# A second expert unit taken straight from SBUF: direct products, outer x sums first, operand streams fetched ahead (fp32 attention, then four experts)

## The chip, the cores and the metric

One core of a Trainium2 chip. The metric is the device time of one execution in microseconds (us); most executions of a kernel agree within 0.3%. A ratio is the mean time of one kernel's fast runs over that of the other's of the same rounds, so it isn't quite the ratio of the medians quoted beside it.

## The reference, cut to what matters

```python
# lightning attention in blocks of 64, with a running state per head
out = intra + inter            # q, k, v: (4, 8, 768, 64) fp32
x = attn_out.transpose(0, 2, 1, 3).reshape(3072, 512)

p = domain_probs / (domain_probs.sum(-1, keepdims=True) + 1e-09)
for e in range(4):             # four experts, all of them on all tokens
    h = np.maximum(x @ w1[e], 0.0)          # 3072x512 @ 512x1024
    out += p[:, e:e + 1] * (h @ w2[e])      # 3072x1024 @ 1024x512
```

## The kernel before

The tokens are taken in three groups g of 1024, and a *unit* (g, e) is one group through one expert. Unit by unit, the second product of one unit (h @ w2) is interleaved on TensorE with the first product (x @ w1) of the next, and with the attention of the next group. Below, "unit 0", "unit 1" and so on without a pair of numbers are the steps of this main loop: unit 0 does the second product of (0,0) and the first of (0,1).

Every product is a Strassen product in Winograd's form: seven products M1 to M7 for eight. The left operands are A11, A12, A22 and the sums S1 to S4 of w1, the right ones B11, B21, B22 and the sums T1 to T4 of x. For the first product this is done twice, an outer level and an inner one. The inner sums are made by GpSimd (w1) and VectorE or GpSimd (x), stored to HBM, and read back as streams:

```python
    def inner(eng, what, to, blk, ops, at):        # four inner sums of one block, then stores
        s = stage.tile([P, 4, 256], FP32, name="ops", tag="st")
        for i, (name, x, y, op) in enumerate(ops):
            b[name] = s[:, SLOT[name]]
            tt(eng, b[name], b[x], b[y], op)
        stores.append(lambda: (
            nc.scalar.dma_start(out=to[:, 0], in_=blk[:, 0, 0:256]),
            nc.scalar.dma_start(out=to[:, 1:5], in_=s[:]),
            nc.scalar.dma_start(out=to[:, 5:7], in_=...), made.add(what)))
    # `stage` has 7 buffers of 4 KB per partition: raw w1 and w2, their sums, x sums, inner sums.

    def feed(g, e, m):                             # both streams of one outer product
        xs = stream.tile([P, 7, 256], FP32, name="xs_in", tag="x")
        nc.sync.dma_start(out=xs[:], in_=x_ops[g, MS.index(m)])
        ws = stream.tile([P, 7, 256], FP32, name="ws_in", tag="w")
        nc.sync.dma_start(out=ws[:], in_=w1_ops[e, MS.index(m)])

    def first_product(...):                        # 7 inner products x 2 matmuls = 14 per outer product
        ...
                nc.tensor.matmul(out=p[...], lhsT=ws[:, W1_AT[i], ...], rhs=xs[:, X_AT[i]], ...)
            # each inner product is taken out of PSUM on its own: 7 evictions of 128x512
```

The very first unit, (0,0), can't wait for such streams. Its products are *direct*: no inner level, operands as they lie in SBUF.

```python
    def direct_product(m, tags):                   # 4 quarters x 4 matmuls = 16 per outer product
        a, b = w1_now[A_OF[m]], x_now[B_OF[m]]
        ...
        def quarter(at):
            for s in range(2):
                for c in range(2):
                    nc.tensor.matmul(out=p[...], lhsT=a[c][:, f:f + P], rhs=b[:, c, ...], ...)
            # 4 evictions of 128x512

    first, own = prepare_w1(1), [lambda x=x: inner_x(nc.vector, 0, x, x_now[B_OF[x]]) for x in SEQ]
    chores.append(first.pop(0))
    for many in zip(own, first):                   # inner sums of x and of w1 of expert 1
        chores.extend(many)
    sum_x("T1", "B12", "B11")
    for m in SEQ0[2:]:                             # M5, M6, M7, M3, M4 of unit (0,0)
        for x, f in enumerate(direct_product(m, (...))):
            f(); rest()
            if x != 2:
                pump()                             # last chore's stores, then the next chore
        if m == "M5":
            sum_x("T2", "B22", "T1")
        if m == "M6":
            sum_x("T3", "B22", "B12")
            sum_x("T4", "B21", "T2")
```

In the traces of this kernel instructions keep their program order on each engine and each queue (in the prediction, one sum on VectorE has its inputs at 71 us and runs at 96.47, behind others); across engines only data and buffers hold them. A buffer goes to the next tile once the last reader of the old one is done (a sum of the changed kernel stood 8.21 us for that).

## Time and profile before

| | before |
|---|---|
| median of 3 runs | 1282.16 us |
| profiled span | 1281.2 us |
| TensorE weight loads busy | 83% |
| VectorE, GpSimd, ScalarE busy | 62%, 23%, 17% |
| TensorE idle from 70 to 145 us | 35.3 us in three waits |
| TensorE idle after 145 us | 4.0 us in seven waits |

A fp32 matmul of 128x128 by 128x256 stands in the trace as two records 0.216 us apart (eight records in 1.73 us), so one matmul is 0.43 us, and "x32" is 16 matmuls. Idle time before a row stands in brackets at its end, with what ended it. In the rows of 40 slices each digit is a share in tenths: of busy time (PE, TensorE) or of the full clock that TensorE was granted (PEclk). PEld are weight loads, DVE is VectorE, ACT ScalarE, POOL GpSimd, and SPq and ACTq are the transfers issued from the sync and the scalar engine. The lines that carry the argument are in the prediction.

### The profile page before, as it was taken

What the parts mean: (1) busy time and instruction counts of PE and PEld (TensorE: products, weight loads), DVE (VectorE), ACT (ScalarE), POOL (GpSimd) and SP (SyncE); (2) the same over time, 40 slices, a digit from 0 to 9 for tenths busy, and PEclk for the clock granted to TensorE, in tenths of its full rate; (3) what the DMA queues carried; (4) which work ended last, traced back from release to release, by engine and by line L of the source; (5) the groups of instructions that cost most, each with busy time, mean ns of one, the idle gap of its engine ahead of it and who ended that gap; (6) DMA issues with size and microseconds to landing.
All of it is one profiled execution on the core that took longest, in us unless ns stands there. A gap on an engine that the chain in (4) does not pass through costs nothing.

```text
span 1281.2 us, 16185 instructions
## 1 busy us (share of the span) xinstructions
PE 1225.6 (96%) x6348; PEld 1069.5 (83%) x6348; DVE 791.5 (62%) x1288; ACT 216.7 (17%) x361; POOL 295.8 (23%) x286
## 2 busy tenths in 40 slices
PE   6967599999999999999999999999999999999998
PEld 5856488888888888888888888888888888888887
DVE  5669357747746855664674684674674764755742
ACT  2211111211221120221121112021020120220200
POOL 3646156057336840011100062000010000000001
PEclk9998699999999999999999999999999999999999
DMA  9747999599979985665754466545374545454412
GB/s 192 215 188 261 291 334 353 191 353 328 334 286 314 325 299 186 195 235 173 230 172 182 163 226 243 217 151 217 150 257 179 204 166 195 174 186 184 164 53 97
DMA packets 173916, 283.85 MB, mean 222 GB/s; under 512 B 87696, under 2 KB 120592, under 8 KB 173840
## 3 DMA queue, kind: packets, MB, share of 16 engines
q1 hardware_dynamic: 144672, 223.11, 51.7%
q10 hardware_dynamic: 27248, 53.41, 11.3%
q0 software_dynamic: 1920, 6.29, 1.3%
q8 instruction: 50, 0.82, 0.3%
q14 instruction: 26, 0.21, 0.0%
HBM read 223.14 MB, written 59.64 MB: 221 GB/s over the span
## 4 chain that ended last, share of the span: by engine, by line
PE 47%; issue 39%; DVE 4%; DMA 4%; POOL 4%; SPq 1%; ACTq 0%; ACT 0%; POOLq 0%; DVEq 0%
PE q L584 19%; PE pg L532 18%; DVE m L93 2%; PE op L384 2%; PE sp L360 2%; PE pM L633 2%; POOL ops L93 2%; PE kvp L393 2%; PE op L378 1%; DMA w_ops<-w1b 1%; PE kp L337 1%; POOL xo L93 1%; DVE ops L93 1%; PE qp L337 1%; DMA ws_in<-w_ops 1%
## 5 line engine op out<-in xcount | busy, mean ns | idle before, releaser
L532 PE MATMUL pg<-xs_in,ws_in 128*128 128x256 f32 x2156 | 520.4, 381 | 25.1 <-DMA ws_in<-w_ops 21.1
L532 PEld LDWEIGHTS pg<-xs_in,ws_in 128*128 128x128 f32 x2156 | 406.7, 190 | 85.0 <-issue 21.8
L93 DVE TENSOR_TENSOR m<-pg,m 128x512 f32<-128x512 f32 x451 | 307.3, 687 | 90.0 <-PE pg L532 82.8
L584 PE MATMUL q<-w2t,hS 128*128 128x256 f32 x1536 | 360.7, 379 | 0.0
L584 PEld LDWEIGHTS q<-w2t,hS 128*128 128x128 f32 x1536 | 291.1, 190 | 39.3 <-issue 0.2
L600 DVE SCALAR_TENSOR_TENSOR acc<-q,gate,acc 128x256 f32<-128x256 f32 x288 | 138.8, 482 | 238.4 <-PE q L584 238.0
L584 PE MATMUL q<-w2t,m 128*128 128x256 f32 x1152 | 270.9, 379 | 0.0
L584 PEld LDWEIGHTS q<-w2t,m 128*128 128x128 f32 x1152 | 219.3, 190 | 29.9
L544 ACT ACTIVATE m<-m 128x512 f32<-128x512 f32 x132 | 82.7, 630 | 381.1 <-DVE m L93 368.8
L602 POOL DMA_DIRECT2D out_dram<-acc x24 | 13.2, 550 | 579.3 <-DVE acc L600 579.3
L93 DVE TENSOR_TENSOR hS<-m,m 128x512 f32<-128x512 f32 x96 | 73.6, 768 | 26.2 <-ACT m L544 26.2
L540 ACT COPY m<-pg 128x512 f32<-128x512 f32 x88 | 51.4, 585 | 208.8 <-PE pg L532 201.1
L93 DVE TENSOR_TENSOR m<-m,m 128x512 f32<-128x512 f32 x96 | 81.1, 846 | 0.0
L93 POOL TENSOR_TENSOR kn<-kn,s_decay 128x256 f32<-128x256 f32 x40 | 29.7, 763 | 158.3 <-PE kp L337 157.1
L597 DVE TENSOR_SCALAR acc<-q,gate 128x256 f32<-128x256 f32 x48 | 23.1, 482 | 51.6 <-PE q L584 51.6
L486 ACT ACTIVATE m<-m 128x512 f32<-128x512 f32 x48 | 30.1, 630 | 144.8 <-DVE m L93 142.8
L93 POOL TENSOR_TENSOR w2o<-w2b 128x1024 f32<-128x1024 f32 x8 | 19.2, 2408 | 104.4 <-DMA w2b<-in_moe_w_dram 104.4
L633 PE MATMUL pM<-xt,w1o 128*128 128x256 f32 x96 | 24.8, 425 | 14.2 <-DVE xt L93 14.2
L388 ACT COPY xT<-op 128x512 f32<-128x512 f32 x24 | 14.0, 584 | 143.6 <-PE op L384 130.2
L93 DVE TENSOR_TENSOR st<-sp,s_decay 128x512 f32<-128x512 f32 x48 | 30.9, 684 | 10.8 <-PE sp L360 10.7
L633 PEld LDWEIGHTS pM<-xt,w1o 128*128 128x128 f32 x96 | 20.6, 217 | 18.2 <-issue 11.9
L93 DVE TENSOR_TENSOR hS<-hS,m 128x512 f32<-128x512 f32 x48 | 35.0, 730 | 0.4
(65 smaller groups left out, 711.6 us busy)
## 6 DMA issues: line engine op xcount, KB each, us to landing
xs_in<-x_ops SPq DMA_DIRECT2D x77, 896.0 KB, 4.7
ws_in<-w_ops SPq DMA_DIRECT2D x77, 896.0 KB, 7.0
w2t<-w_sums SPq DMA_DIRECT2D x96, 256.0 KB, 6.5
w2t<-in_moe_w_dram SPq DMA_DIRECT2D x72, 256.0 KB, 4.9
w_ops<-ops ACTq DMA_DIRECT2D x28, 512.0 KB, 4.6
x_ops<-ops ACTq DMA_DIRECT2D x21, 512.0 KB, 3.7
w2b<-in_moe_w_dram SPq DMA_DIRECT2D x32, 256.0 KB, 7.5
w_sums<-w2o ACTq DMA_DIRECT2D x16, 512.0 KB, 7.1
```

Of the source, the lines that this page charges most:

```text
L93: eng.tensor_tensor(out=o, in0=a, in1=b, op=op)
L337: nc.tensor.transpose(out=x[:, hp * C:(hp + 1) * C], in_=y[:, 2 * hp:2 * hp + 2].rearrange("p h d -> p (h d)"), identity=ident[:],)
L360: nc.tensor.matmul(out=sp[hd][:, hp * C:(hp + 1) * C], lhsT=hc(kT)[half[hd], hp], rhs=hc(qT)[half[hd], hp], start=True, stop=True,)
L384: nc.tensor.matmul(out=op[half[hd], hp * C:(hp + 1) * C], lhsT=vn[:, 2 * hp + hd], rhs=hc(st[hd])[:, hp], start=(first and hp == 0), stop= ...
L393: nc.tensor.matmul(out=kpv[:, hp], lhsT=kn[:, 2 * hp:2 * hp + 2].rearrange("p h d -> p (h d)"), rhs=vn[:, 2 * hp:2 * hp + 2].rearrange("p ...
L486: nc.scalar.activation(out=o[:], in_=o[:], func=AF.Relu)
L532: nc.tensor.matmul(out=p[:, j * 256:(j + 1) * 256], lhsT=ws[:, W1_AT[i], j * P:(j + 1) * P], rhs=xs[:, X_AT[i]], start=(fresh and j == 0), ...
L540: nc.scalar.copy(out=new[at][:], in_=p[:])
L544: nc.scalar.activation(out=new[at][:], in_=new[at][:], func=AF.Relu)
L584: nc.tensor.matmul(out=p[:, s * DH:(s + 1) * DH], lhsT=h[A_OF[m]][:, c * 256 + s * P:c * 256 + (s + 1) * P], rhs=fed2[g, e, m][uu][:, c], ...
L600: nc.vector.scalar_tensor_tensor(out=o, in0=x, scalar=w, in1=o, op0=ALU.mult, op1=ALU.add)
L633: nc.tensor.matmul(out=p[:, s * 256:(s + 1) * 256], lhsT=a[c][:, f:f + P], rhs=b[:, c, j * 256:(j + 1) * 256], start=(s == 0 and c == 0), ...
```

## The change

The intent: unit (0,1) is made direct as well, so that nothing has to come through HBM before unit (0,2); its raw w1 is loaded and the sums of it are begun during unit (0,0), the inner x blocks are made during unit 0's second product, and all four T sums are made before anything else on VectorE. The streams are asked for one product ahead across the border of two units.

```diff
     sum_x("T1", "B12", "B11")
+    sum_x("T2", "B22", "T1")
+    sum_x("T3", "B22", "B12")
+    sum_x("T4", "B21", "T2")
     for f in between:
         f()
+    chores.extend(lambda n=n: raw_w1(1, n) for n in ("A11", "A12", "A21", "A22"))
+    chores.append(lambda: sum_w1(1, "S1", "A21", "A22", ALU.add))
     for m in SEQ0[2:]:
-        for x, f in enumerate(direct_product(m, (...))):
+        for x, f in enumerate(direct_product(0, m, blocks, (...))):
             f(); rest()
-            if x != 2:
+            if x == 1:
                 pump()
-        if m == "M5": ...                          # T2 here, T3 and T4 after M6
+    own = [lambda m=m: inner_x(nc.vector, 0, m, x_now[B_OF[m]]) for m in SEQ0]
+    w2_steps, w1_steps = prepare_w2(1), prepare_w1(2)
+    chores.extend((                                # done during unit 0
+        lambda: sum_w1(1, "S2", ...), own[0], lambda: sum_w1(1, "S3", ...), own[1], w2_steps[0],
+        lambda: sum_w1(1, "S4", ...), own[2], w2_steps[1],
+        own[3], w2_steps[2], w2_steps[3], own[4], w2_steps[4], w1_steps[0], own[5], *w1_steps[1:3], own[6], *w1_steps[3:],
+    ))
...
+    fill = [(*u, m) for u in units[2:] for m in SEQ]
+    fill2 = [(*u, m) for u in units for m in SEQ2]
     for at, (g, e) in enumerate(units):
-        feed2(g, e, SEQ2[0])
         for i in range(7):
-            if i + 1 < 7:
-                feed2(g, e, SEQ2[i + 1])
+            for _ in range(2 if at + i == 0 else 1):
+                if fill2:
+                    feed2(*fill2.pop(0))
             b = second_product(g, e, SEQ2[i], banks)
-            if ahead:
-                feed(*ahead, SEQ[i])
+            if at == 0:
+                a = direct_product(1, SEQ0[i], blocks, ("g1", "g3"))
+            elif ahead:
                 a = first_product(*ahead, SEQ[i], blocks, ("g1", "g3"))
...
-                if ahead and x == 0 and i + 1 < 7:
-                    feed(*ahead, SEQ[i + 1])
+                if x == 0 and at * 7 + i >= 6 and fill:
+                    feed(*fill.pop(0))
```

Cut: w1 of expert 1 for the later groups is prepared in unit 3, four attention steps go from unit 0 to units 1 and 2, and the loads of two attention chunks go into unit 0.

More of the change, by code (lines that the diff above doesn't have):

```diff
@@ L258, with raw_w1, sum_w1 @@
     make_identity(nc, ident[:])
-    w1_now = {}
-    def raw_w1(name):
+    w1_now = {0: {}, 1: {}}
+    def raw_w1(e, name):
         i, j = int(name[1]) - 1, int(name[2]) - 1
         if name == "A22":
-            w1_now[name] = tuple(small("w1b")[:] for _ in range(2))
+            to = tuple(small("w1b")[:] for _ in range(2))
         else:
             t = stage.tile([P, 2, W], FP32, name="w1b", tag="st")
-            w1_now[name] = t[:, 0], t[:, 1]
+            to = t[:, 0], t[:, 1]
         for c in range(2):
             r = j * 256 + c * P
-            nc.sync.dma_start(out=w1_now[name][c], in_=moe_w1[0, r:r + P, i * W:(i + 1) * W])
-    def sum_w1(name, a, b, op):
-        w1_now[name] = tuple(small("w1o")[:] for _ in range(2))
+            nc.sync.dma_start(out=to[c], in_=moe_w1[e, r:r + P, i * W:(i + 1) * W])
+        w1_now[e][name] = to
+    def sum_w1(e, name, a, b, op):
+        if e == 0:
+            to = tuple(small("w1o")[:] for _ in range(2))
+        else:
+            t = stage.tile([P, 2, W], FP32, name="w1o", tag="st")
+            to = t[:, 0], t[:, 1]
         for c in range(2):
-            tt(nc.gpsimd, w1_now[name][c], w1_now[a][c], w1_now[b][c], op)
+            tt(nc.gpsimd, to[c], w1_now[e][a][c], w1_now[e][b][c], op)
+        w1_now[e][name] = to
     for n in range(4):
         load(n)
-    raw_w1("A21")
-    raw_w1("A22")
-    raw_w1("A11")
+    for name in ("A21", "A22", "A11"):
+        raw_w1(0, name)
     probs = consts.tile([P, NTOK // P, E], FP32, name="probs")
@@ L615, with direct_product @@
     SEQ0 = ("M1", "M2", "M5", "M6", "M7", "M3", "M4")
-    blocks = {}
     x_now = {"B11": b11, "B21": b21, "B12": b12, "B22": b22}
     turns = itertools.count()
-    def direct_product(m, tags):
-        a, b = w1_now[A_OF[m]], x_now[B_OF[m]]
+    def direct_product(e, m, blocks, tags):
+        a, b = w1_now[e][A_OF[m]], x_now[B_OF[m]]
         settle(m, blocks)
@@ L643, in quarter @@
                 nc.scalar.activation(out=new[at][:], in_=new[at][:], func=AF.Relu)
-        return [lambda at=at: quarter(at) for at in ("11", "12", "21", "22")] + [lambda: finished(0, 0, m, blocks, new)]
+        return [lambda at=at: quarter(at) for at in ("11", "12", "21", "22")] + [lambda: finished(0, e, m, blocks, new)]
     pairs = (("s0", "s1"), ("q01", "q02"), ("q11", "q12"))
-    between = []
+    between, blocks = [], {}
     for i in range(CPG + 2):
         if i == 3:
-            sum_w1("S1", "A21", "A22", ALU.add)
-            sum_w1("S3", "A11", "A21", ALU.subtract)
+            sum_w1(0, "S1", "A21", "A22", ALU.add)
+            sum_w1(0, "S3", "A11", "A21", ALU.subtract)
         if i == 4:
-            sum_w1("S2", "S1", "A11", ALU.subtract)
-            sum_w1("S4", "A12", "S2", ALU.subtract)
+            sum_w1(0, "S2", "S1", "A11", ALU.subtract)
+            sum_w1(0, "S4", "A12", "S2", ALU.subtract)
             chores.extend(prepare_w2(0))
@@ L660 @@
         if i == 6:
-            between = direct_product("M1", ("g1", "g3"))
+            between = direct_product(0, "M1", blocks, ("g1", "g3"))
         for f, lag in ((scores, 1), (turn, 0), (values, 2)):
@@ L666 @@
             if i == 7 and lag == 0:
-                between += direct_product("M2", ("g1", "g3"))
+                between += direct_product(0, "M2", blocks, ("g1", "g3"))
             if between:
@@ L672 @@
         if i == 0:
-            raw_w1("A12")
+            raw_w1(0, "A12")
         if i == 6:
@@ L680, in sum_x @@
         tt(nc.vector, x_now[name], x_now[a], x_now[b], ALU.subtract)
-    first, own = prepare_w1(1), [lambda x=x: inner_x(nc.vector, 0, x, x_now[B_OF[x]]) for x in SEQ]
-    chores.append(first.pop(0))
-    for many in zip(own, first):
-        chores.extend(many)
     sum_x("T1", "B12", "B11")
+    sum_x("T2", "B22", "T1")
+    sum_x("T3", "B22", "B12")
+    sum_x("T4", "B21", "T2")
     for f in between:
         f()
+    chores.extend(lambda n=n: raw_w1(1, n) for n in ("A11", "A12", "A21", "A22"))
+    chores.append(lambda: sum_w1(1, "S1", "A21", "A22", ALU.add))
     for m in SEQ0[2:]:
-        for x, f in enumerate(direct_product(m, ("g1", "g3", "q01", "q02", "q11", "q12"))):
+        for x, f in enumerate(direct_product(0, m, blocks, ("g1", "g3", "q01", "q02", "q11", "q12"))):
             f()
             rest()
-            if x != 2:
+            if x == 1:
                 pump()
-        if m == "M5":
-            sum_x("T2", "B22", "T1")
-        if m == "M6":
-            sum_x("T3", "B22", "B12")
-            sum_x("T4", "B21", "T2")
-    for n in range(CPG, CPG + AHEAD):
-        load(n)
+    own = [lambda m=m: inner_x(nc.vector, 0, m, x_now[B_OF[m]]) for m in SEQ0]
+    w2_steps, w1_steps = prepare_w2(1), prepare_w1(2)
+    chores.extend((
+        lambda: sum_w1(1, "S2", "S1", "A11", ALU.subtract), own[0],
+        lambda: sum_w1(1, "S3", "A11", "A21", ALU.subtract), own[1], w2_steps[0],
+        lambda: sum_w1(1, "S4", "A12", "S2", ALU.subtract), own[2], w2_steps[1],
+        own[3], w2_steps[2], w2_steps[3], own[4], w2_steps[4], w1_steps[0], own[5], *w1_steps[1:3], own[6], *w1_steps[3:],
+    ))
     units = [(g, e) for g in range(NG) for e in range(E)]
+    fill = [(*u, m) for u in units[2:] for m in SEQ]
+    fill2 = [(*u, m) for u in units for m in SEQ2]
     steps = attention(1)
     for at, (g, e) in enumerate(units):
-        if g == 0 and e < E - 1:
+        if (g, e) == (0, 1) or (g, e) == (0, 2):
             chores.extend(prepare_w2(e + 1) + prepare_w1((e + 2) % E))
+        if (g, e) == (0, 3):
+            chores.extend(prepare_w1(1))
         ahead = units[at + 1] if at + 1 < len(units) else None
@@ L712 @@
         blocks, banks = {}, {}
-        feed2(g, e, SEQ2[0])
         for i in range(7):
-            if i + 1 < 7:
-                feed2(g, e, SEQ2[i + 1])
+            for _ in range(2 if at + i == 0 else 1):
+                if fill2:
+                    feed2(*fill2.pop(0))
             b = second_product(g, e, SEQ2[i], banks)
             a = []
-            if ahead:
-                feed(*ahead, SEQ[i])
+            if at == 0:
+                a = direct_product(1, SEQ0[i], blocks, ("g1", "g3"))
+                a = a[0:1] + [None] + a[1:2] + [None] + a[2:3] + [None] + a[3:]
+            elif ahead:
                 a = first_product(*ahead, SEQ[i], blocks, ("g1", "g3"))
@@ L724 @@
                 for f in part:
-                    f()
+                    if f:
+                        f()
                 rest()
-                if ahead and x == 0 and i + 1 < 7:
-                    feed(*ahead, SEQ[i + 1])
-                if steps and (x == 5 or (x == 2 and i in (2, 5))):
+                if x == 0 and at * 7 + i >= 6 and fill:
+                    feed(*fill.pop(0))
+                if at == 0 and x == 0 and i < AHEAD:
+                    load(CPG + i)
+                if steps and (at > 0 or i > 1) and (x == 5 or (x == 2 and i in (1, 3, 5) and at > 0)):
                     steps.pop(0)()
```

## The prediction

> **What bounds the kernel now.** I read the page's rows of 40 slices first, then who TensorE waited for, then the stretch with the waits in order of time, then the queue that feeds it.
>
> ```profile
> PE   6967599999999999999999999999999999999998
> PEclk9998699999999999999999999999999999999999
> ```
>
> One slice is 32 us. TensorE is full from the sixth slice on; what can be won without removing matmuls lies in the first five, about 160 us.
>
> ```profile
> PE pg L532 <- DMA ws_in<-w_ops: 21.1, 1, 21.1
> PE pM L633 <- DVE xt L93: 14.2, 2, 11.5
> PE qp L337 <- DMA qn<-in_q_dram: 7.1, 2, 4.7
> PE pg L532 <- DVE m L93: 4.0, 7, 0.9
> ```
>
> These are TensorE's waits over the whole span: total, times, longest. The loads at the start (7.1) are not touched by the change. One wait of 21.1 us for a transfer and two for the outer x sums (11.5 and 2.7) make 35.3 us. The timeline places them:
>
> ```profile
> 72.67 15.77 PE L633 MATMUL pM<-xt,w1o 128*128 128x256 f32 x64 [2.66 <-DVE xt L93]
> 99.98 9.06 PE L633 MATMUL pM<-xt,w1o 128*128 128x256 f32 x32 [11.54 <-DVE xt L93]
> 108.87 7.07 PE L633 MATMUL pM<-xT,w1o 128*128 128x256 f32 x32
> 115.78 7.07 PE L633 MATMUL pM<-xt,w1b 128*128 128x256 f32 x32
> 143.97 3.75 PE L532 MATMUL pg<-xs_in,ws_in 128*128 128x256 f32 x8 [21.12 <-DMA ws_in<-w_ops]
> ```
>
> Columns: start, length, operation and count, and in brackets the idle time before it and who ended it. L633 is the direct product of unit (0,0): M5 and M6 in the first row, then M7, M3, M4. L532 is the first product of unit (0,1) from operands that went through HBM. From 72.67 to 143.97, 71.3 us, TensorE does only five direct products.
>
> The sync queue's view of the same stretch says why the transfer is late:
>
> ```profile
> 98.77 0.37 SPq L176 DMA_DIRECT2D w1b<-in_moe_w_dram  x1
> 122.22 0.37 SPq L103 DMA_DIRECT2D qn<-in_q_dram  x1
> 134.96 0.36 SPq L467 DMA_DIRECT2D ws_in<-w_ops  x1
> ```
>
> The queue issues nothing between 99.1 and 122.2, then the attention loads and the w2 blocks, and only at 134.96 the operands that TensorE needs. Ahead of that, GpSimd and VectorE must make inner operand blocks of w1 and x, and the scalar queue must store them. VectorE's own lines show that the 11.5 us are no dependency but a place in a queue:
>
> ```profile
> 71.38 1.23 DVE L93 TENSOR_TENSOR xt<-xT 128x1024 f32<-128x1024 f32 x1
> 93.02 1.80 DVE L93 TENSOR_TENSOR ops<-xT 128x256 f32<-128x256 f32 x2
> 94.86 1.69 DVE L93 TENSOR_TENSOR ops<-xT,ops 128x256 f32<-128x256 f32 x2
> 96.47 3.35 DVE L93 TENSOR_TENSOR xt<-xT 128x1024 f32<-128x1024 f32 x1
> ```
>
> The T3 sum at 96.47 has had its inputs (xT) since 71, but stands behind `ops` work in VectorE's order.
>
> **What the Trainium skill says.** "Perfetto Trace Analysis", section Identifying the Most-Contended Engine: matmul busy time is a poor measure of headroom; weight-load busy time is a better one. The trace agrees and gives the scale:
>
> ```profile
> 800.00:900.00 100.00, 100.00 (x465) 88.04 (x464) 60.24 (x102) 14.76 (x24) 0.00 (x0) 1.00 0.51 189
> 72.67:143.97 71.30, 38.63 (x160) 32.77 (x161) 50.05 (x67) 9.37 (x16) 32.95 (x28) 0.79 0.76 270
> ```
>
> (Stretch and length, then busy us of PE, PEld, DVE, ACT, POOL, granted clock, DMA share, GB/s.) A full 100 us has 88.04 of weight loads. The 32.77 of the stretch are therefore worth 32.77/0.8804 = 37.2 us, so 34.1 us are to be had.
>
> "TensorE: Matmul & The Clock Gate", Part 1: an idle window of about 3.4 us puts the array to half clock until it has been busy for about as long. The trace agrees: the first eight records after the 21.1 us gap take 3.75 us, and eight in full flow 1.73; the stretch's granted clock is 0.79.
>
> "SBUF — State Buffer", Who interferes with whom: a VectorE instruction with two SBUF inputs and a GpSimd instruction that reads SBUF exclude each other. The trace agrees: the same xt sum takes 1.23 us at 71.38 and 3.35 at 96.47 beside GpSimd; the eviction with one input in PSUM stays at 0.687. So the T sums gain twice by going first.
>
> **The change part by part.** *Outer x sums first.* T1 to T4 now follow each other on VectorE at 71.4. T1 still ends at about 72.6, so the wait of 2.66 stays; T2, T3, T4 end near 73.9, 75.1 and 76.3, long before M6, M7 and M4 want them. The wait of 11.54 goes.
>
> *Direct phase of unit (0,0).* It now holds only evictions, ReLUs, hidden sums and loads of the second unit's raw w1. Each product is 32 records at 1.73/8 = 0.216, or 6.91 us; five make 34.6, and I add 2.0 because the first comes off the 2.66 gap (M5's 32 records take 8.88 in the chain of waits, not 6.91). VectorE: 16 evictions, 12 block adds and some 8 hidden sums at 0.69, with T2 to T4, 28 to 29 us of 36.6: not the bound, though 80%. The phase should end near 109.3.
>
> *Unit (0,1) direct.* Its operands are already in SBUF, so neither w1_ops nor x_ops stands before it. The 21.12 goes, with the cold start behind it (3.75 - 1.73 = 2.0) and 0.3 in the next eight. So the 71.3 us become 36.6: **-34.7**, and **-2.3** for the cold start. (By weight loads I had 34.1 for the first.)
>
> *More matmuls.* Direct is 16 matmuls of 256 columns per outer product, 32 records, against 14 and 28 with the inner level. Seven products: 28 records more, 28 x 0.216 = **+6.05**, all of it on TensorE, which is full there. VectorE has 28 evictions for 49, worth 21 x 0.687 = 14.4 us of its time, but it is not the bound in unit 0, so this is only slack. The bank of a quarter also gets a longer time to empty (about two quarters and two second-product parts, 4 x 1.73, less the own matmuls) than an inner product's.
>
> *Moved work.* The inner x blocks (7 x 4 sums at about 0.43 alone = 12 us of VectorE), their stores, w2 of expert 1 and w1 of expert 2 now run inside unit 0 behind 104 us of matmuls; w1 of expert 1 moves to unit 3, which had no such work. Four attention steps move from unit 0 to units 1 and 2; each takes the same TensorE time there. Old unit 0 had two small waits, 0.34 and 0.66, each with 0.26 of a slower restart: **-1.5**.
>
> *Fetching ahead across units.* Small effect: after 225 us TensorE never waits for a transfer before, only 3.0 us for VectorE. I count 0.
>
> Sum without new waits: -34.7 - 2.3 + 6.05 - 1.5 = -32.4, or 1249.7 us.
>
> **The rivals.** (a) *The stage buffers become the wait.* Seven buffers now hold the second unit's raw and summed w1 together with the x blocks and the w2 sums. In the third outer product of unit 0 (M5) I count S2, S3, S4 (direct operands still to come), B12, B22, B11 and T3 of w2: seven. The fourth x block, on VectorE, then has to wait until T3 is summed and stored (w_sums stores take 7.1 us median from issue to landing). I put it at about 8 to 10 us of blocked VectorE; the next product's evictions stand behind it, and TensorE can run some 7 us further on two banks. That leaves a gap of 2 to 4 us, perhaps with a cold restart. For it: VectorE, scalar and sync queues showed waits on just such stores in before (the sync queue waited 29.3 us on w_ops<-w1o). I take **+4**, which puts the time at 1254. If it repeats at the fifth and sixth block, or the 47 small buffers run short too, it is +10 or more: about 1262.
>
> (b) *The wait moves.* The first operands of unit (0,2) still need x_ops and w1_ops through HBM, at the start of unit 1. But they are made by the sixth product of unit 0 and fetched in the seventh, 13.8 us before use, against 4.7 and 7.0 us from issue to landing. It would make 1265; I hold it unlikely.
>
> (c) *No new wait at all*, 1250. For it: VectorE has 60 to 66% load in unit 0 and evictions are fewer.
>
> (d) *More clashes in unit 3 and at the group change*, where GpSimd now makes w1 of expert 1 beside attention; the waits at 407 to 450 in before (2.8 us) show the size: 0 to +2, which I leave to the range and out of the centre.
>
> **Range and chances.** Centre 1253.5 us, between (c) and a light (a). A faster end of 1247 needs the waits at 407 to 450 to go too; the slow end of 1266 holds a heavy (a) or (b). Two per cent is 1256.5, so new waits of under 6.8 us give a clear gain: 0.68. Within 2%: 0.31. Slower by 2% would need waits of over 58 us: 0.01.
>
> **What would show it.** Right: TensorE's wait list without ws_in and with one xt wait near 2.7; the last L633 records of the first unit ending near 109; 224 more records of direct product and 196 fewer of L532; some waits of 1 to 4 us of TensorE for VectorE in 135 to 160, behind an `ops` sum that waited for a store. Wrong: a new wait for ws_in near 210, or gaps in the direct phase (raw w1 late or VectorE too slow), or a sum of small waits in units 0 to 3 above 7 us.

## More of the kernel before

The runs fell on several chips: the kernel before took 1281.49 us (median) on the first, and 1279.71, 1282.05 and 1282.13 beside the three groups of experiments. Kernels of different groups are therefore compared by their ratios to it.

## The result, and the profile after

The changed kernel took 1259.37 us (median of 4 runs, 1257.37 to 1262.57) against 1281.49 for the kernel before in the same rounds: ratio 0.983, 95% interval 0.9807 to 0.9852. That is 1.7% less, within the range of the prediction and 6 us above its centre. It misses the gain of 2% to which the prediction had given a chance of 0.68. The profiled span went from 1281.2 to 1257.4 us, -23.8.

The rows of 40 slices and TensorE's waits (total, times, longest) of the changed kernel:

```profile
PE   6989999999999999999999999999999999999998
PEclk9999999999999999999999999999999999999999
```

```profile
PE qp L342 <- DMA qn<-in_q_dram: 8.4, 3, 4.7
PE pg L537 <- DVE m L93: 3.4, 4, 1.8
PE pM L637 <- DVE xt L93: 3.3, 1, 3.3
PE pg L537 <- ACT m L545: 3.1, 2, 2.2
PE sp L365 <- ACT kT L348: 3.0, 3, 1.7
...
PE pM L637 <- DVE m L93: 1.5, 1, 1.5
```

The 21.1 us for `ws_in` and the 11.5 us for `xt` are gone. What remains are many short waits for VectorE and ScalarE, where the kernel before had 4.0 us in all after 145 us. TensorE's rows where the five direct products of unit (0,0) turn into unit 0's main loop:

```profile
73.82 22.67 PE L637 MATMUL pM<-xt,w1o 128*128 128x256 f32 x96 [3.28 <-DVE xt L93]
96.33 7.07 PE L637 MATMUL pM<-xT,w1o 128*128 128x256 f32 x32
103.23 7.07 PE L637 MATMUL pM<-xt,w1b 128*128 128x256 f32 x32
110.14 1.89 PE L637 MATMUL pM<-xT,w1b 128*128 128x256 f32 x8
111.87 1.89 PE L589 MATMUL q<-w2t,m 128*128 128x256 f32 x8
```

Five products, then at 110.14 the first quarter of unit (0,1) with nothing between. Unit (0,1) began at 143.97 before; that is 33.8 us less.

Two of the new waits show how they come about. First the start of the direct phase, 1.15 us later than before. T1 on VectorE, and what GpSimd did in that time:

```profile
72.05 1.72 DVE L93 TENSOR_TENSOR xt<-xT 128x1024 f32<-128x1024 f32 x1
```

```profile
67.37 2.67 POOL L93 TENSOR_TENSOR w1o<-w1b 128x512 f32<-128x512 f32 x2 [5.79 <-DMA w1b<-in_moe_w_dram]
70.02 2.66 POOL L93 TENSOR_TENSOR w1o<-w1o,w1b 128x512 f32<-128x512 f32 x2
```

T1 takes 1.72 us for 1.23 before. GpSimd holds S2 of the second unit's w1 until 72.68, 0.63 us into T1, which is longer by 0.5; in the kernel before GpSimd did nothing from 70.2 to 78.8. These early w1 sums belong to the change: they are listed as chores of unit 0, but nothing holds GpSimd back until then. The Trainium skill, "SBUF — State Buffer", Who interferes with whom, says that a VectorE sum of two SBUF inputs, as T1 is, and a GpSimd instruction that reads SBUF contend, and this trace agrees: 0.5 us more beside 0.63 us of GpSimd. (The rest of the delay, some 0.65 us, is mostly upstream: the last attention matmuls of group 0 began 0.53 us later, at 69.38. A load of q held TensorE up for 1.29 us in this run, but the repeat in experiment 8 has no such wait and begins its direct phase at 73.84 all the same, so the cause stays open.)

Second, the wait that the prediction's first rival had named. VectorE, then TensorE:

```profile
158.29 0.76 DVE L93 TENSOR_TENSOR ops<-xt 128x256 f32<-128x256 f32 x2 [8.21 <-DMA w_sums<-w2o]
...
161.01 1.35 PE L637 MATMUL pM<-xt,w1o 128*128 128x256 f32 x5 [1.49 <-DVE m L93]
```

The fourth inner x block (`ops`) stood 8.21 us on VectorE until the store of a w2 sum had landed and freed a stage buffer. The evictions behind it were late, and TensorE, which ran on for most of that time on its other bank, lost 1.49 us.

### The profile page after: what moved, and what is told of

The parts are those of the page before. It is cut to its first block, busy times and chain, and to the rows that moved or that the text cites. A ratio compares the mean times of both kernels' runs of the same rounds, so it can differ in the third digit from the quotient of the medians.

```text
span 1257.4 us, 16224 instructions
## 1 busy us (share of the span) xinstructions
PE 1226.8 (98%) x6376; PEld 1071.3 (85%) x6376; DVE 762.4 (61%) x1267; ACT 217.1 (17%) x361; POOL 301.1 (24%) x294
## 4 chain that ended last, share of the span: by engine, by line
PE 47%; issue 42%; DMA 5%; POOL 2%; SPq 2%; DVE 1%; ACT 0%; ACTq 0%; POOLq 0%; DVEq 0%
PE q L589 18%; PE pg L537 14%; PE pM L637 7%; PE op L389 2%; PE sp L365 2%; PE kvp L398 2%; SPq L103 1%; PE op L383 1%; DMA xs_in<-x_ops 1%; DMA x_ops<-xo 1%; DMA w2t<-in_moe_w_dram 1%; POOL ops L93 1%; POOL out_dram L607 1%; PE qp L342 1%; DMA kn<-in_k_dram 1%
## 5 line engine op out<-in xcount | busy, mean ns | idle before, releaser
L537 PE MATMUL pg<-xs_in,ws_in 128*128 128x256 f32 x1960 | 470.9, 380 | 6.6 <-DVE m L93 3.4
L537 PEld LDWEIGHTS pg<-xs_in,ws_in 128*128 128x128 f32 x1960 | 369.2, 190 | 60.3 <-DVE m L93 5.6
L93 DVE TENSOR_TENSOR m<-pg,m 128x512 f32<-128x512 f32 x410 | 280.1, 688 | 92.9 <-PE pg L537 79.2
L549 ACT ACTIVATE m<-m 128x512 f32<-128x512 f32 x120 | 75.4, 630 | 361.9 <-DVE m L93 349.7
L93 DVE TENSOR_TENSOR hS<-m,m 128x512 f32<-128x512 f32 x96 | 68.8, 719 | 20.9 <-ACT m L549 20.9
L545 ACT COPY m<-pg 128x512 f32<-128x512 f32 x80 | 46.5, 585 | 174.9 <-PE pg L537 157.1
L93 DVE TENSOR_TENSOR m<-m,m 128x512 f32<-128x512 f32 x96 | 73.8, 773 | 0.0
L491 ACT ACTIVATE m<-m 128x512 f32<-128x512 f32 x48 | 29.9, 629 | 152.3 <-DVE m L93 147.7
L637 PE MATMUL pM<-xt,w1o 128*128 128x256 f32 x192 | 45.6, 391 | 4.8 <-DVE xt L93 3.3
L637 PEld LDWEIGHTS pM<-xt,w1o 128*128 128x128 f32 x192 | 37.2, 196 | 10.7 <-DVE xt L93 3.5
L93 DVE TENSOR_TENSOR m<-pM,m 128x512 f32<-128x512 f32 x40 | 27.4, 687 | 24.9 <-PE pM L637 24.8
```

What stands on the lines that cost most here:

```text
L93: eng.tensor_tensor(out=o, in0=a, in1=b, op=op)
L491: nc.scalar.activation(out=o[:], in_=o[:], func=AF.Relu)
L537: nc.tensor.matmul(out=p[:, j * 256:(j + 1) * 256], lhsT=ws[:, W1_AT[i], j * P:(j + 1) * P], rhs=xs[:, X_AT[i]], start=(fresh and j == 0), ...
L545: nc.scalar.copy(out=new[at][:], in_=p[:])
L549: nc.scalar.activation(out=new[at][:], in_=new[at][:], func=AF.Relu)
L637: nc.tensor.matmul(out=p[:, s * 256:(s + 1) * 256], lhsT=a[c][:, f:f + P], rhs=b[:, c, j * 256:(j + 1) * 256], start=(s == 0 and c == 0), ...
```

## The experiments

Eleven kernels were run, all but one with correct results.

### 1. The T sums first, and nothing else

```diff
 # the kernel before
     sum_x("T1", "B12", "B11")
+    sum_x("T2", "B22", "T1"); sum_x("T3", "B22", "B12"); sum_x("T4", "B21", "T2")
...
-        if m == "M5": sum_x("T2", ...)
-        if m == "M6": sum_x("T3", ...); sum_x("T4", ...)
```

> The kernel before with one part of the change: T1 to T4 made together before the direct products, all else as before. Theory: the 11.5 us wait for xt goes, but the operands of unit (0,1) are still made by the same chain on GpSimd, VectorE and the store queue, which is not shortened, so most of the time comes back as a longer wait for ws_in: that wait grows from 21.1 to 28 us or more, and the time stays within 5 us of 1281.5. Rival (the two waits are independent and add): the ws_in wait stays near 21 us and the time falls by the 11.5 us and about 1.5 us of cold restart, to about 1268.

Measured: 1278.24 us, ratio 0.9984 (0.9966 to 1.0002). TensorE's waits, and its rows, of this kernel:

```profile
PE pg L532 <- DMA ws_in<-w_ops: 23.9, 1, 23.9
...
PE pM L633 <- DVE m L93: 3.6, 1, 3.6
```

```profile
109.84 7.13 PE L633 MATMUL pM<-xt,w1b 128*128 128x256 f32 x32
140.84 3.75 PE L532 MATMUL pg<-xs_in,ws_in 128*128 128x256 f32 x8 [23.87 <-DMA ws_in<-w_ops]
```

The 11.5 us wait is gone, and the last direct product ends near 117 instead of 122.9. But the operands of unit (0,1) come at 140.84 instead of 143.97: most of the time saved is now spent in a longer wait for `ws_in` (23.9) and a new one for an eviction (3.6), with a cold restart behind it. I had put the longer wait at 28 or more, which was too much, but the time says what the theory said: two waits in a row on one chain don't add. Taking away the first alone was worth about 2 us by the ratio, whose interval runs from 4.4 us to nothing (`ws_in` came 3.1 us earlier in the trace).

### 2. The changed kernel with the T sums late

```diff
 # the changed kernel
-    sum_x("T2", ...); sum_x("T3", ...); sum_x("T4", ...)     # ahead of the products
+        if m == "M5": sum_x("T2", ...)
+        if m == "M6": sum_x("T3", ...); sum_x("T4", ...)
```

> The changed kernel with only the T sums put back to their old places (T2 after M5, T3 and T4 after M6). Theory: what held T3 back in the kernel before was the inner x blocks ahead of it on VectorE, and these have left the direct phase; so a wait for xt of 2 to 3 us at M7 at most, and 1261 to 1264 us against 1259.4. Rival (the order of the T sums is itself a main part of the gain): a wait near 10 us and 1269 or more.

Measured: 1262.78 us, ratio 0.9868 (0.985 to 0.9885). The waits for `xt` sum to 6.5 us in two (3.92 and 2.61), for one of 3.28:

```profile
92.07 7.15 PE L637 MATMUL pM<-xt,w1o 128*128 128x256 f32 x32 [2.61 <-DVE xt L93]
```

Against the 0.983 and 0.9819 of the changed kernel the order of the sums is worth 0.4 to 0.5%, 5 to 6 us by the ratios, but its interval overlaps that of the first (0.9807 to 0.9852). In the traces the first output row of group 1 is begun at 551.84, for 548.98 in the changed kernel and 547.84 in its second run (experiment 8), so 3 to 4 us is the safer figure. That is more than the ratio gave the same edit in experiment 1, where what stood behind it gave the time back; with these intervals the difference isn't shown. As expected it isn't near 10 us: what had held T3 back was the inner x work on VectorE, and that has left this phase.

### 3. What the extra matmuls cost

```diff
 # the changed kernel, wrong result on purpose
-                for c in range(2):
+                for c in range(1 if e == 1 and at == "22" else 2):
```

> Wrong result on purpose: the second unit's direct products leave out 2 of their 16 matmuls, so that their count is that of the inner Strassen level (14), all else as in the changed kernel. Theory: TensorE is full in this stretch, the extra 28 records at 0.216 us are paid in full, so the time falls by 5.5 to 6.5 us, to about 1253.4. Rival (evictions or the buffer waits set the pace there): it falls by less than 3 us.

Measured: 1253.67 us, ratio 0.9799 (0.978 to 0.9817); the relative error of the result was 0.096, as intended. Against 0.983 and 0.9819 that is 0.2 to 0.3%, 2.6 to 4 us, less than expected and on both sides of the rival's mark; the ratios don't decide. In the trace the first output row of group 1 is begun at 543.48, for 548.98 in the changed kernel and 547.84 in its second run (experiment 8), 4.4 to 5.5 us earlier, although this run had two losses of its own: a colder start of the direct phase (the first 96 records took 23.84 us for 22.67) and a wait of 1.49 us for VectorE at 203 us. Unit 0 alone, from its first direct record to the first one of the streamed operands, shows it more closely. The two ends in the changed kernel, then in this one:

```profile
110.14 1.89 PE L637 MATMUL pM<-xT,w1b 128*128 128x256 f32 x8
215.94 1.89 PE L537 MATMUL pg<-xs_in,ws_in 128*128 128x256 f32 x8
```

```profile
111.45 1.89 PE L637 MATMUL pM<-xT,w1b 128*128 128x256 f32 x8
212.50 1.89 PE L537 MATMUL pg<-xs_in,ws_in 128*128 128x256 f32 x8
```

That is 105.80 and 101.05 us. The waits in it, with 0.26 of slower restart each, are one of 1.49 and two of 1.00 and 1.49; without them 104.05 and 98.04 are left. So TensorE did have the 6.0 us less to do, and a new wait took back over 1 us of them: the extra matmuls are paid in full, and the evictions don't set the pace.

### 4. Without fetching ahead

```diff
 # the changed kernel
+        feed2(g, e, SEQ2[0])                       # w2 tiles unit by unit, as before
...
+            if at > 0 and ahead: feed(*ahead, SEQ[i])
...
-                if x == 0 and at * 7 + i >= 6 and fill:
-                    feed(*fill.pop(0))
+                if at > 0 and ahead and x == 0 and i + 1 < 7:
+                    feed(*ahead, SEQ[i + 1])
```

> The changed kernel with the streams of operands fetched in the old order: w2 tiles and the xs/ws pairs are asked for unit by unit, nothing ahead across the border of two units. Theory: no effect beyond 2 us, since in the kernel before TensorE never waited for a transfer after 145 us. Rival: at the start of unit 1 the first operand pair is asked for too late, as it was at the start of unit (0,1) before; a wait of 5 to 20 us for ws_in or xs_in near 210 us, 1265 to 1280.

Measured: 1266.56 us, ratio 0.99 (0.9882 to 0.9918). The theory fell and the rival holds. The sync queue of the changed kernel around the start of unit 1, then the sync queue and TensorE of this one:

```profile
200.47 0.34 SPq L472 DMA_DIRECT2D ws_in<-w_ops  x1
211.87 0.38 SPq L176 DMA_DIRECT2D w1b<-in_moe_w_dram  x1
```

```profile
211.13 0.37 SPq L176 DMA_DIRECT2D w1b<-in_moe_w_dram  x1
...
216.01 0.34 SPq L472 DMA_DIRECT2D ws_in<-w_ops  x1
```

```profile
224.50 3.75 PE L537 MATMUL pg<-xs_in,ws_in 128*128 128x256 f32 x8 [9.13 <-DMA ws_in<-w_ops]
```

In the changed kernel the first `ws_in` leaves at 200.47, ahead of the `w1b` load that has to wait for a buffer until 211.87. In the old order it stands behind that load and the four w2 loads after it, leaves at 216.01, and TensorE waits 9.13 us for it, with a cold restart (3.75 us for eight records). A second wait of 2.11 us follows later. Fetching ahead, which I had counted as nothing, is worth 9 to 10 us within this change (0.99 against 0.983 and 0.9819): without it the wait removed at the start of unit 0 comes back at the start of unit 1 at near half its size.

### 5. GpSimd's stores on GpSimd's own queue

```diff
 # the changed kernel; stores of what GpSimd made
-            nc.scalar.dma_start(out=to[:, 1:5], in_=s[:]),
+            nc.gpsimd.dma_start(out=to[:, 1:5], in_=s[:]),   # and the like for w1, x, w2 sums
```

> The changed kernel, but what GpSimd makes (inner blocks of w1 and x, w2 sums) is stored from GpSimd's own queue, no longer from the scalar engine's. Theory: of the small waits left in the changed kernel, those at 237, 308, 444 and 484 us (0.85, 1.67, 2.24 and 1.81, with 0.26 of slower restart each, 7.6 us in all) come from stores that stand in the scalar engine's order and wait for GpSimd, with copies out of PSUM behind them; they go, and the time falls by 4 to 7 us to 1252 to 1255. Rival (VectorE and GpSimd getting in each other's way, or buffers, make these waits): they stay, within 2 us of 1259.4, or slower since GpSimd now spends time on issuing.

Why I tried it, in the scalar engine's rows of the changed kernel, where the copies out of PSUM (L545) and the stores stand in one order:

```profile
437.05 0.36 ACTq L146 DMA_DIRECT2D x_ops<-xT  x1
437.43 0.59 ACT L545 COPY m<-pg 128x512 f32<-128x512 f32 x1
440.29 0.33 ACTq L147 DMA_DIRECT2D x_ops<-ops  x1
443.20 0.33 ACTq L148 DMA_DIRECT2D x_ops<-xT  x1
443.57 0.58 ACT L545 COPY m<-pg 128x512 f32<-128x512 f32 x1 [5.55 <-DMA x_ops<-xo]
```

Three stores take from 437.05 to 443.5 because they wait for GpSimd's sums and for earlier transfers, and before the copy at 443.57 ScalarE stands idle for 5.55 us; TensorE waits 2.24 us for that copy.

Measured: 1268.67 us, ratio 0.9897 (0.9884 to 0.9911), slower than the changed kernel by 0.7 to 0.8%. TensorE's waits:

```profile
PE pg L538 <- DVE m L93: 8.0, 9, 1.6
...
PE pM L638 <- DVE m L93: 3.2, 2, 2.9
...
PE sp L366 <- ACT kT L349: 1.4, 2, 0.7
```

The cause fits and the remedy was wrong. Every wait for ScalarE after the first 20 us is gone (the 1.4 left lie in the first 17), but the waits for VectorE rose from 3.4 and 1.5 us to 8.0 and 3.2. GpSimd now spends about 0.54 us on each of 142 issues, and its VectorE neighbour's two-input sums are longer (for instance 0.811 for 0.719 us mean in the largest group of hidden sums). From the last output's issue to the end of the program it also took 6.8 us instead of 4.1. The stages of the two traces place the 9.2 us between the spans: unit 0 took 112.2 us for 105.8 (its waits for VectorE are 2.86, 0.36, 1.67 and 0.52 us, the first with a cold restart), from there to group 1 the kernel gained 1.9, after it lost 1.7, and 2.7 are the end. So the remedy helped a little where it was aimed, and lost more in unit 0.

### 6. Eight stage buffers

```diff
-    stage = ctx.enter_context(tc.tile_pool(name="stage", bufs=7))
+    stage = ctx.enter_context(tc.tile_pool(name="stage", bufs=8))
```

> The changed kernel with 8 stage buffers for 7, nothing else. Theory (the first rival of the prediction): the fourth x block no longer waits 8.2 us for the store of a w2 sum, the wait of 1.49 us at 161 us goes with its slower restart, and the time falls by 1.5 to 3 us. Rival: the wait only moves to the next store or to the scalar engine's queue, and the time is the same within 1 us.

Measured: 1255.05 us, ratio 0.9784 (0.977 to 0.9797): faster than before by more than 2%, and 4 to 6 us better than the changed kernel by the ratios. TensorE's waits:

```profile
PE pM L637 <- DVE xt L93: 3.6, 1, 3.6
...
PE pg L537 <- ACT m L545: 2.2, 1, 2.2
PE pg L537 <- DVE m L93: 2.1, 4, 0.9
...
PE pM L637 <- DVE m L93: 1.0, 1, 1.0
```

The gain is larger than expected. VectorE's 8.21 us wait for a buffer is gone (0.5 us is left there), and so are not only the 1.49 us at 161 but also the waits at 237, 308 and 484 us, which I had put down to the order of stores alone. The stores were late partly because what they stored had waited for a buffer. The waits after 112 us fall from 9.6 to 5.3 us. Where I expected the gain there is hardly any: unit 0 takes 105.5 us for 105.8, since a new wait of 0.97 us at 208 comes in place of the 1.49. The 4 us are won between there and group 1, by the waits that I hadn't laid to the buffers.

### 7. The same two remedies in the kernel before

The edits of experiments 5 and 6, each alone in the kernel before:

```diff
 # first kernel: the inner sums of x and w1 that GpSimd made, and its w2 sums
+        by = nc.gpsimd if eng is nc.gpsimd else nc.scalar
-            nc.scalar.dma_start(out=to[:, 1:5], in_=s[:]),
+            by.dma_start(out=to[:, 1:5], in_=s[:]),          # and the like
 # second kernel
-    stage = ctx.enter_context(tc.tile_pool(name="stage", bufs=7))
+    stage = ctx.enter_context(tc.tile_pool(name="stage", bufs=8))
```

> The kernel before with GpSimd's stores from its own queue. Theory: the 21 us wait for ws_in comes from the whole chain of making operands of which GpSimd's sums (about 50 us from 67 to 120) are the longest part, so the wait shortens by a few us only, to 12 to 20, and the time to 1270 to 1279. Rival (the order of the scalar engine's queue alone made the operands late): the wait falls under 6 us and the time to 1264 or less.

Measured: 1291.87 us, ratio 1.0078 (1.0064 to 1.0091). The wait for `ws_in` fell from 21.1 to 17.6 us, as expected, but the time rose instead of falling: the waits for evictions grew (10.8 us in twelve for 4.0 in seven), and those for `xt` hardly changed (13.5 for 14.2). I hadn't foreseen that.

> The kernel before with 8 stage buffers for 7. Theory: the chain of making operands is bound by GpSimd and VectorE work more than by buffers; the wait for ws_in falls by less than 8 us, time 1272 or more. Rival (the chain was slow because its steps waited for buffers): the wait falls by 12 us or more, time under 1268.

Measured: 1284.35 us, ratio 1.0018 (1.0005 to 1.0032); `ws_in` 20.7 us, `xt` 13.0. So before the change an eighth buffer was worth nothing, and it is worth 5 us after it. The late operands of unit (0,1) were neither a matter of one buffer nor of GpSimd's stores in the scalar queue alone (more buffers, and both remedies together, weren't tried); what removed the wait was to need no such operands there.

### 8. The changed kernel again, and two versions that go further

```diff
 # the 8-buffer kernel
+            if n == CPG - 1: late.append(update)   # attention state of chunk 7: after T1 on VectorE
+            else: update()
...
+            elif old is None and (g, e, m) == (1, 0, "M1"):
+                nc.vector.tensor_copy(out=new[at][:], in_=p[:])   # ScalarE stands behind stores here
```

The last kernel has the same two edits, 9 stage buffers, and 45 small buffers for 47 to pay for them.

> The changed kernel once more, unaltered, on the same chip and in the same rounds as the next two, so that these can be compared with it directly: 1257 to 1262 us, ratio to before near 0.983. Seven stage buffers: again a wait of 1 to 2 us at about 161 us, where the fourth x block waits for the store of a w2 sum.

> A version meant to beat both: the changed kernel with 8 stage buffers, the update of the attention state of chunk 7 put behind T1 on VectorE (nothing needs it before unit 0), and the first product of group 1 (M1) copied out of PSUM by VectorE, since the scalar engine stands behind stores there. Theory: against the 8-buffer run (ratio 0.9784) the wait for xt at 74 us falls from 3.6 to about 2 with less of a cold start, 1.4 to 2 us; the wait of 2.2 us at 442 with its 0.3 of restart goes; so 1250 to 1252 us, ratio 0.975 to 0.977. Rival: the waits only move to the next store or eviction, and the ratio stays at 0.978.

> The version before with 9 stage buffers, paid for by 45 small buffers instead of 47. Theory: with 8 the only wait for a buffer on TensorE's path was gone, so a ninth brings nothing: within 1.5 us of the run before. Rival: stage buffers still hold back the x and w1 blocks and with them the scalar engine's stores, so 2 to 4 us more are won; or the small buffers now run short and it loses some us.

| | median us | ratio | 95% interval |
|---|---|---|---|
| changed kernel again | 1258.35 | 0.9819 | 0.9806 to 0.9833 |
| 8 buffers and two edits | 1250.84 | 0.9754 | 0.9741 to 0.9767 |
| 9 buffers and two edits | 1248.92 | 0.9747 | 0.9734 to 0.9761 |

The changed kernel repeats its time, and the wait at 161 us (1.25 this time). Both edits do what they were made for: with 8 buffers TensorE's wait for `xt` falls to 0.9, with 0.7 for the update moved behind it, the wait at 442 is gone, and the ratio is at the good end of the expected span. The ninth buffer changes the ratio by less than its interval, as the theory had it. These two are the best versions here, 2.5% faster than the kernel before.

They also bear on when the cold start comes. Granted clock (third column from the end) in stretches of 2 us, for the changed kernel, where TensorE had waited 3.28 us, and for the 9-buffer kernel, where it had waited 1.95:

```profile
74.00:76.00 2.00, 2.00 (x7) 1.64 (x8) 2.00 (x2) 0.00 (x0) 0.00 (x0) 0.65 0.58 131
76.00:78.00 2.00, 2.00 (x7) 1.53 (x6) 2.00 (x4) 0.58 (x1) 0.00 (x0) 0.50 0.00 0
```

```profile
74.00:76.00 2.00, 2.00 (x11) 1.77 (x11) 2.00 (x2) 0.63 (x2) 0.00 (x0) 1.00 0.00 0
76.00:78.00 2.00, 2.00 (x11) 1.77 (x10) 2.00 (x4) 0.91 (x2) 0.00 (x0) 1.00 0.56 229
```

After 1.95 us of waiting the first 96 records took 21.07 us, after 3.28 they took 22.67, 1.6 us more. The length of the wait doesn't settle it alone: after the 2.66 us of the kernel before the clock was 0.50 from 74 to 76 us, but after the 2.61 us of experiment 2 (row at 92.07) it stayed at 1.00.

## Why the prediction was right or wrong

The time lay inside the range, and most terms of the sum came out as written. The mechanism held; the term for new waits was too small, and the value of one part was put in the wrong place.

- **Direct phase, -34.7.** Measured -33.8. The five products took 36.3 us for a predicted 36.6, cold start included. They began 1.15 us later: 0.5 because the second unit's w1 sums on GpSimd ran into T1, the rest mostly upstream. I had said that the T sums gain by going first, and had not asked what else would now run at that time.
- **Cold restart after the `ws_in` wait, -2.3.** It is gone: unit 0 begins at full rate. It was worth 2.2: the prediction took 1.73, a distance from start to start, from 3.75, the length of a row; from start to start these eight records took 3.55.
- **More matmuls, +6.05.** 28 records more of TensorE work, paid in full (experiment 3: 6.0 us of unit 0 without its waits; net of other waits 2.6 to 4 us by the ratios, 4.4 to 5.5 in the trace at group 1).
- **Small waits.** This is the term that was mis-sized. I had taken away 1.5 us and added 4 for rival (a), +2.5. Measured: before, 4.0 us in seven waits with 0.26 of slower restart each, 5.8 in all; after, 9.6 us in eight with 1.9 of restarts, 11.5; so +5.7. Rival (a) itself came as described: the fourth x block, held for 8.21 us (predicted 8 to 10) by the store of a w2 sum; its direct price was smaller, 1.5 us for 2 to 4. That the 4 us set down for it came close at all was luck: other waits filled them. The rest came from places that I hadn't followed: stores in the scalar engine's order, with PSUM copies behind them, at 237, 308, 444 and 484 us. Experiment 6 shows that three of these four go with one more stage buffer, so the rival was right and drawn too small. It also shows that I was wrong to look for it only at the block where the count of buffers first went over seven.
- **The sum.** -33.8 - 2.2 + 6.05 + 5.7 = -24.2, against -23.8 of the two spans.
- **Fetching ahead, 0.** Wrong, by the reasoning that TensorE never waited for a transfer after 225 us in the kernel before. That trace had its one such wait at the start of the first streamed unit, and the change moves this start to unit 1. I had even used the early fetch to dismiss rival (b), and not noticed that it was this part which dismissed it. Without it, (b) comes true (experiment 4: 9.13 us, 9 to 10 us of time). The total wasn't hurt, since the kernel has the fetch.
- **The chance of 0.68 for over 2%.** It stood on new waits below 6.8 us over a base of 1249.7. The small waits alone were 3.2 us above what I had allowed, and the later start took 1.15; that is most of the 6 us between the centre and the result. Two per cent was within reach of one more buffer.

## What to carry to other kernels

Waits in a row on one chain of making operands needn't add (they didn't in experiment 1): take away the need for the chain, then see to the order of what feeds the next place that needs it, or the wait comes back there. When a change parks more tiles in a shared pool of buffers, count the tiles that live at each step and try one buffer more before anything else; the same buffer may have been worth nothing in the kernel before. In a queue that keeps its order, a request that may have to wait for a buffer should stand behind the requests that the busiest engine needs soon.

## What the Trainium skill lacked or had wrong

- "TensorE: Matmul & The Clock Gate", Part 1, puts the return to half clock at an idle window of about 3.4 us. Here waits of 2.66 us (before) and 3.28 us (after) were enough: granted clock 0.50 in a stretch of 2 us afterwards, and 96 records in 22.67 us after the longer one for 21.07 after 1.95 us. Waits of 1.95 us and, in experiment 2, 2.61 us left the clock at 1.00. No single mark to stay under comes out of these runs.
- The same page's Back-to-back issue gap has no figure for fp32 (the number of passes of a fp32 product stands elsewhere in the skill; its time and its look in a trace don't). Here a fp32 matmul with 256 columns is two records of 0.216 us each, 0.43 us, with a weight load of 0.19 us for each record hidden behind it.
- "DMA: Bandwidth & Descriptors", Issuing engines are not separate DMA queues, says that issuing from several engines saves only the issue time. That section gives no measure of what the order in the issuing engine does: a load waiting for a buffer held the requests behind it on the same queue back until TensorE stood for 9.13 us, and stores issued by ScalarE left it idle for 5.55 us with a PSUM copy behind them. To move the stores to GpSimd made the kernel 0.7 to 0.8% slower.
